# QK-norm attention and a SiLU feed-forward on one core: three more couples of heads loaded in 32-row quarters and transposed on VectorE

## The chip, the core and the metric

The kernel runs on one core of one Trainium2 chip. TensorE (PE in the profile) multiplies matrices and writes PSUM; VectorE (DVE), ScalarE (ACT) and GpSimd (POOL) do the rest; DMAs are issued from queues, nearly all of them here from the SyncE queue (SP). The metric is the time of one execution on the device in microseconds (us); lower is better.

## The reference

```python
def rmsnorm(x, g):                       # over the 64 columns of a head
    return x / np.sqrt(np.mean(x * x, axis=-1, keepdims=True) + 1e-06) * g
q_n, k_n = rmsnorm(q, g_q), rmsnorm(k, g_k)       # (8, 12, 448, 64) each
scores = (1 / 8) * np.matmul(q_n, k_n.transpose(0, 1, 3, 2))
attn = softmax(scores)                            # + 1e-9 in the denominator
attn_out = np.matmul(attn, v)
x = attn_out.transpose(0, 2, 1, 3).reshape(3584, 768)
h = x @ w_in                                      # w_in (768, 2048)
out = (h / (1 + exp(-h))) @ w_out                 # w_out (2048, 768)
```

q, k, v and the gains are float32. `w_in` and `w_out` come as 64-bit floats, which the kernel loads as pairs of 32-bit words and rounds to float32 itself.

## The kernel before

**Couples.** The 12 heads of each of the 8 batches are worked on four at a time. Such a set of four heads is a *couple*; there are 24 (`NC`), three to a batch, so couple c belongs to batch c // 3. The main loop of `bounded` runs over c and calls `visit(c)` and then `between(c)`.

`visit(c)` holds the attention matmuls of couple c: `scores` (keys by queries into a PSUM tile `sc`, then ScalarE's Exp, L731) alternates with `weigh` (exponentials by v, L763). It also divides the couple before by its softmax sums (`divide`, L824), and in some couples it rounds a piece of `w_in` (`weights_in_visit`).

`between(c)` prepares couple c + 1 and fills TensorE's time with the feed-forward of two batches that are finished. It runs `fill` twice. A `fill` takes a fixed number of steps of the feed-forward's matmuls (L923; one step is one float32 product of 448 columns, two instructions in the trace): 13 steps in couples 6 to 11, 14 from couple 12 on. Among these steps `fill` deals out other work by hand: a list `others`, spread evenly over the steps, and a list `prompt`, of which one entry is issued at once and one more after every third step. The matmuls are those of a seven-product scheme (`Seven`): products 1, 2, 6, 5, 7, 3, 4 of three steps each make one block; product 5 is copied to a `stage` slot by ScalarE (L941), product 1 too (L931), the others are added by VectorE (L873), GpSimd adds two parts (L943, L944), and when a block is done ScalarE applies SiLU (L1061) and SP stores it to `hidden` (L956). There are three `stage` slots, so product 5 of a block goes into a slot whose store must have landed.

**Two ways to normalise and transpose.** Before the scores, q and k must stand with the 64 columns of a head on partitions.

- Couples 6 to 11, below `LATE` (12): q is loaded by rows (L266, two DMAs of 224 KB) and k by rows (L292, L296, four DMAs). Squares are taken by ScalarE (L470) and summed by VectorE (L471); GpSimd takes the power -1/2 (L499) and multiplies q (L514); for k the factor is used later as the scale of the Exp. `transpose_q` is 8 TensorE transposes (L643) and a ScalarE copy of 128x896 (L647); `transpose_k` is 7 transposes (L661) and a ScalarE copy that applies the gains (L663).
- Couples from `LATE` on: q is loaded in 32-row quarters (`load_quarters`, L253, eight DMAs of 56 KB with runs of 32 floats), and k twice, by rows for its squares (L285, L287, six DMAs) and in quarters (L253, eight more). v comes in plain token order (L312, L323, L325: eight DMAs instead of four). `flip` transposes 32x32 blocks on VectorE (L669 for q, L672 for k); `gain` applies the gains to k (ScalarE, L678). The squares of q are one ScalarE instruction (`sum_squares`, L686) and one VectorE sum (L687); `scale` adds the two halves of a head with a small TensorE matmul (L698), and VectorE (L699) and GpSimd (L702 power, L705 multiply) finish. `pair_up` changes the identity matrix for that matmul once, two couples ahead.

In the `between` of these late couples the second `fill` has this list of prompts: the first reciprocal of the softmax sums (L808) at once; the second and its spreading DMAs (L815, L817) after step 3; `flip(c + 1, "k")` and the load of the next quarters after step 6; `gain` and `sum_squares(c + 2)` after step 9. After the last step `scale(c + 2)` is issued, so its matmul L698 stands on TensorE between the feed-forward and the scores of `visit(c + 1)`. The weight steps of that `fill` are dealt in its first half, since as many empty entries are put behind them.

**Buffers and banks.** From couple 8 on, q has one buffer, so the load of the next q is issued behind the transposition of the present one. The places `k0` and `k1` hold k of even and odd couples below `LATE`; from there on `k0` takes the rows and `k1` the quarters. `bank` gives the feed-forward's products their PSUM: two `mm` banks, and, when `turns["third"]` is set (c >= `LATE` - 1), every other product takes an `sc` tile instead while more than five steps are due.

**The weights.** `w_in` is 24 pieces: a load (L86, SP), an opening by ScalarE (L101, L102; "o" in the table of steps) and a rounding by VectorE (L124, L127, L131) and GpSimd (L135; "r"). The last ones fall into couples 6 to 10, and so do the sums of weight blocks for the seven products (`sum_w_in`, L870 and L873 on W, 128x768): four in the visits of couples 7 and 9, and in couple 10 three in the first `fill` and one in the second. A load into a raw buffer waits on SP until the piece before it there has been rounded.

**The order of the output.** Up to `plain` = 4, batches hold their tokens with every fourth token side by side, and `store` writes a tile of 128 tokens in two or three interleaved DMAs (L533); from batch 4 on in one or two plain ones (L526).

Of the kernel before, what the change touches and what calls it, by code (L numbers as in the profile page):

```python
# [30 lines left out]
class Shapes:  # L31
    def __init__(self, q, w_in):
        self.B, self.H, self.S, self.D = q.shape
        self.DM, self.DFF = w_in.shape
        self.P = 128
        self.J = 4
        self.R = self.S // self.J
        self.NPAIR = self.H // 2
        self.NW = self.DM // self.P
        self.NF = self.DFF // self.P  # L40
        self.HALF = self.DM // 2
        self.FULL = self.S // self.P
        self.REST = self.S - self.FULL * self.P

        self.KEYS = self.S // self.P
        self.LEFT = self.S - self.KEYS * self.P
        assert 2 * self.LEFT == self.P and self.NPAIR % 2 == 0 and self.LEFT == self.D

        self.KA, self.KL, self.KB = 0, 2 * self.KEYS * self.D, 2 * (self.KEYS + 1) * self.D
        self.NK = self.KB + 2 * self.KEYS * self.D  # L50
        assert 2 * self.D == self.P and self.J * self.R == self.S and 2 * self.REST == self.P
        assert self.NW == self.NPAIR and self.B % 2 == 0

        self.LATE = 2 * self.NPAIR
        self.Q = 32
        assert 2 * self.S == self.NK and 4 * self.Q == self.P and self.D == 2 * self.Q

# [136 lines left out]
def kernel(  # L194
# [25 lines left out]
    nc = tc.nc  # L220
    z = Shapes(q, w_in)
# [8 lines left out]
    place, at = {}, 0  # L230
# [16 lines left out]
    def load_quarters(rows, t):  # L247

        rows = rows.rearrange("n (a p) d -> n p a d", p=z.Q)
        for i in range(2):  # L250
            for h, half, quarter in z.quarters():
                dst = t[quarter, ts(i, z.S)].rearrange("p (a e) -> p a e", e=z.Q)
                nc.sync.dma_start(dst, rows[2 * i + h][:, :, ts(half, z.Q)])  # L253
# [18 lines left out]

    def load_k_quarters(c):
        b, cp = divmod(c, z.NPAIR // 2)
        load_quarters(k[b, ts(cp, 4)], place["k1"])

    def load_k(c):
        t = place[f"k{c % 2}"]
        if c >= z.LATE:
            t = place["k0"]  # L280
            for i, start in enumerate((z.KA, z.KB)):
                main, left = plain(k, c, i)
                dst = t[:, ds(start, z.KL)].rearrange("p (j h d) -> p h j d", j=z.KEYS, h=2)
                for h in range(2):
                    nc.sync.dma_start(dst[:, h], main[:, h])  # L285
                dst = t[ds(i * z.LEFT, z.LEFT), ds(z.KL, 2 * D)]
                nc.sync.dma_start(dst.rearrange("p (h d) -> p h d", h=2), left)  # L287
            return
        main, left = keys_of(k, c)
        for i, start in enumerate((z.KA, z.KB)):  # L290
            dst = t[:, ds(start, z.KL)].rearrange("p (j h d) -> p j h d", j=z.KEYS, h=2)
            nc.sync.dma_start(dst, main[:, ts(i, 2)].rearrange("p h j d -> p j h d"))  # L292
            if i == 0:
                for m in range(2):
                    dst = t[ds(m * z.LEFT, z.LEFT), ds(z.KL, 2 * D)]
                    nc.sync.dma_start(dst.rearrange("p (h d) -> p h d", h=2), left[m])  # L296

    def plain(source, c, i):

        b, cp = divmod(c, z.NPAIR // 2)  # L300
        rows = source[b, ds(4 * cp + 2 * i, 2)]
        start = i * z.LEFT
        main = rows[:, ds(start, z.KEYS * P)].rearrange("h (j p) d -> p h j d", p=P)
        return main, rows[:, ds((1 - i) * z.KEYS * P, z.LEFT)].rearrange("h p d -> p h d")
# [56 lines left out]
    norm = Norm(nc, z, rms, minus_half)  # L361
# [177 lines left out]
def bounded(  # L539
# [10 lines left out]
    NC, loads, place, norm, spare, ones, first, squares = (  # L550
        own[name] for name in ("NC", "loads", "place", "norm", "spare", "ones", "first", "squares")
    )
    GROUP, LATE = z.NPAIR, z.LATE
# [13 lines left out]
    def piece(n):  # L567
        nonlocal at
        at += n
        return work[:, at - n : at]  # L570

    qT = piece(2 * S).rearrange("p (i s) -> p i s", i=2)
    kT = piece(z.NK)
# [26 lines left out]
    def q_of(c):  # L600
        return rows_q[c % 2 if c < GROUP + 2 else 0]
# [64 lines left out]
    def flip(c, name):  # L666

        if name == "q":
            nc.vector.transpose(qT.rearrange("p i s -> p (i s)"), q_of(c)[:, 0 : z.NK])  # L669
            load_q(c + 1)  # L670
            return
        nc.vector.transpose(kT, place["k1"])  # L672
        if c + 1 < NC:
            loads["quarters"](c + 1)

# [152 lines left out]
    def normalise(c):  # L828


        def piece(name, i):
            t = scratch[i if c < GROUP + 2 else 0]
            source = raw_of(c) if c < GROUP else q_of(c)
            if name == "q":
                norm.squares_q(c, source, t, i)
            else:
                norm.squares_k(c, place["k0" if c >= LATE else f"k{c % 2}"], t, i)
            if name == "q" and c < GROUP:
                norm.root(c, name, i)
                norm.scale(c, source, q_of(c), i, nc.gpsimd)  # L840
                if i == 1 and c + 2 < GROUP:
                    load_q(c + 2)
            elif i == 1:
                norm.root(c, name)
                if name == "q":
                    for m in range(2):
                        norm.scale(c, source, q_of(c), m, nc.gpsimd)
                elif LATE <= c < NC - 1:
                    loads["k"](c + 1)

        if c >= NC:
            return []
        return [lambda a=a: piece(*a) for a in (("q", 0), ("q", 1), ("k", 0), ("k", 1))]
# [261 lines left out]
    QUADS = NT // 4  # L1115
    QUARTER = z.HALF // 2
# [156 lines left out]
    def save_out(q, i, j):  # L1273
        for t in range(2):
            store(
                nc, out, z, (4 * q + 2 * (i - 1) + t) * P, results[i, j][t], (j - 1) * z.HALF,
                nc.gpsimd if q == QUADS - 1 and i == 2 else nc.sync, plain=4,
            )

    def quad(q):  # L1280
        c = results

        def product(name, out, more):
            n = DEEP.index(name)
            if q > 0 or n >= FIRST:
                deep(name, out, more, DEEP[(n + 1) % len(DEEP)])
                return
            for t in range(2):
                o = single(name, t)
                if more:  # L1290
                    plus(o, out[t], out[t])
                else:
                    nc.scalar.copy(out[t], o)

        first = q == 0
        if first:
            fetch(0, 1, 0)
            sum_deep_right(7)
        product(4, c[2, 1], False)
        if first:  # L1300
            sum_deep_right(4)
        sum_left(0)
        sum_left(2)
        if first:
            sum_deep_right(3)
        product(1, c[1, 1], False)
        for t in range(2):
            nc.scalar.copy(c[1, 2][t], c[1, 1][t])
        sum_left(1)
        if first:  # L1310
            sum_deep_right(6)
            sum_deep_right(1)
        product(2, c[1, 1], True)
        save_out(q, 1, 1)
        if first:
            sum_deep_left(6)
            sum_deep_right(2)
        sum_left(3)
        product(5, c[2, 2], False)
        if first:  # L1320
            owed.extend(lambda i=i: sum_deep_right(5, (i,)) for i in ORDER)
        fetch(q + 1, 1, 1)
        product(6, c[1, 2], True)
        fetch(q + 1, 0, 0)
        product(7, aside, False)
        for t in range(2):
            plus(aside[t], c[1, 2][t], aside[t])
            plus(c[1, 2][t], c[2, 2][t], c[1, 2][t])
            plus(c[2, 2][t], aside[t], c[2, 2][t])
            plus(c[2, 1][t], aside[t], c[2, 1][t])  # L1330
        save_out(q, 2, 2)
        save_out(q, 2, 1)
        fetch(q + 1, 1, 0)
        if q == QUADS - 1:

            def then(t, h):
                store(
                    nc, out, z, (4 * q + t) * P, c[1, 2][t][:, ts(h, QUARTER)],
                    z.HALF + h * QUARTER, *((nc.scalar, nc.sync)[:: 1 if h else -1]), plain=4,
                )  # L1340

            deep(3, c[1, 2], True, None, then)
            return
        product(3, c[1, 2], True)
        save_out(q, 1, 2)
        fetch(q + 1, 0, 1)
# [457 lines left out]
```

## Time and profile before

| | us |
|---|---|
| median of 3 runs | 1311.59 (1311.17 to 1312.17) |
| the profiled execution | 1311.68 |
| its span, first to last instruction | 1309.9 |
| TensorE busy | 1294.2 (99% of the span) |
| VectorE / ScalarE / GpSimd busy | 950.1 / 505.0 / 360.8 |
| DMAs of queue q1 (SP) | 38.8% of 16 engines' span |

Times inside the span are counted from its start. Couple c runs from the first score matmul of `visit(c)` to that of `visit(c + 1)`: couple 7 starts at 150.45, 8 at 184.66, 9 at 218.56, 10 at 251.88, 11 at 287.69, 12 at 319.65. Busy time of TensorE is not throughput: the profile models the ends of matmuls, and one that follows another begins before the modelled end of the first. So the distances between starts are what counts here, and the chain of waits shows these. A queue of an engine (SPq) shows DMA issues, which aren't counted as busy.

### The profile page before, as it was taken

To read this page: it belongs to the slowest core of one execution; us is meant where nothing else is said; L and a number is where in the kernel's file an instruction comes from. 1 tells how busy PE (TensorE), PEld (TensorE's weight loads), DVE (VectorE), ACT (ScalarE), POOL (GpSimd) and SP (SyncE) were. 2 spreads that over 40 slices of the span, in tenths; PEclk is the share of its full clock that TensorE was granted. 3 is DMA by queue.
4 is the path that set the end of the run, shared out by engine and by line. 5 is a ranking of instruction groups with operands and counts; after the bars stand their busy time and mean duration, and the time that the engine had idled before them with its cause. 6 is when DMAs were issued, how large, how long until landed. Compare 5 with 4: busy or idle time off the path is not lost.

```text
span 1309.9 us, 19866 instructions
## 1 busy us (share of the span) xinstructions
PE 1294.2 (99%) x7209; PEld 832.3 (64%) x7209; DVE 950.1 (73%) x1627; ACT 505.0 (39%) x886; POOL 360.8 (28%) x230
## 2 busy tenths in 40 slices
PE   9999999999999999999999999999999999999998
PEld 4444444444444444444444455558999999999998
DVE  6998777777655556755554786698978787878785
ACT  7866656645544545545544354310000000100000
POOL 6766544453334333334320244300000000000000
PEclk9999999999999999999999999999999999999999
DMA  9674335344443444444321457312323223231411
GB/s 242 169 198 121 100 98 164 113 95 110 108 94 90 121 96 95 98 113 95 83 68 63 141 191 253 125 61 78 106 81 101 85 95 110 68 127 52 136 42 40
DMA packets 249439, 144.94 MB, mean 111 GB/s; under 512 B 184292, under 2 KB 233220, under 8 KB 249332
## 3 DMA queue, kind: packets, MB, share of 16 engines
q1 hardware_dynamic: 248672, 142.42, 38.8%
q8 instruction: 59, 0.97, 0.3%
q0 software_dynamic: 352, 0.96, 0.2%
q14 instruction: 48, 0.39, 0.1%
q10 hardware_dynamic: 308, 0.20, 0.1%
HBM read 93.98 MB, written 41.29 MB: 103 GB/s over the span
## 4 chain that ended last, share of the span: by engine, by line
PE 94%; DVE 2%; ACT 2%; issue 1%; POOL 0%; ACTq 0%; DVEq 0%; POOLq 0%
PE alone L1230 23%; PE mm L923 22%; PE av L763 9%; PE sc L726 9%; PE sc L923 9%; PE mm L1230 8%; PE alone L923 7%; PE alone L1267 2%; PE sc L799 1%; PE mm L799 1%; PE mm L1267 1%; PE sc L643 1%; PE sc L661 1%; ACT work L731 1%; DVE work L777 0%
## 5 line engine op out<-in xcount | busy, mean ns | idle before, releaser
L731 ACT ACTIVATE work<-sc,rms 128x448 f32<-128x448 f32 x318 | 181.1, 634 | 63.1 <-PE sc L726 50.4
L923 PE MATMUL mm<-x,W 128*128 128x448 f32 x414 | 169.9, 545 | 4.0 <-DVE parts L873 1.8
L726 PE MATMUL sc<-work 64*64 64x448 f32 x1344 | 164.1, 544 | 1.8 <-ACT work L731 1.5
L777 DVE TENSOR_TENSOR work<-work 128x896 f32<-128x896 f32 (+1 forms) x114 | 124.6, 1125 | 50.0 <-PE av L763 49.5
L923 PE MATMUL mm<-sums_x,W 128*128 128x448 f32 x372 | 152.5, 543 | 0.5 <-DVE parts L873 0.5
L763 PE MATMUL av<-work,rows 64*64 64x448 f32 x1272 | 150.7, 540 | 0.5 <-DVE av L739 0.3
L499 POOL TENSOR_TENSOR rms<-rms,minus_half 128x14 f32<-128x14 f32 (+4 forms) x43 | 105.4, 2453 | 148.2 <-DVE rms L495 138.6
L923 PEld LDWEIGHTS mm<-x,W 128*128 128x128 f32 x414 | 76.4, 190 | 87.2 <-issue 73.7
L526 POOL DMA_DIRECT2D out_dram<-x x2 | 1.2, 592 | 443.3 <-DVE x L873 443.3
L923 PEld LDWEIGHTS mm<-sums_x,W 128*128 128x128 f32 x372 | 69.2, 190 | 73.7 <-issue 68.0
L1230 PE MATMUL alone<-W,rows 128*128 128x192 f32 x610 | 113.0, 326 | 0.0
L763 PEld LDWEIGHTS av<-work,rows 64*64 64x64 f32 x1272 | 57.8, 132 | 69.1 <-issue 33.8
L1230 PEld LDWEIGHTS alone<-W,rows 128*128 128x128 f32 x610 | 101.5, 190 | 0.0
L726 PEld LDWEIGHTS sc<-work 64*64 64x64 f32 x1344 | 52.9, 132 | 74.1 <-ACT work L731 30.8
L943 POOL TENSOR_TENSOR parts<-parts,stage 128x448 f32<-128x448 f32 x31 | 41.9, 1351 | 146.7 <-DVE parts L873 146.3
L923 PE MATMUL sc<-x,W 128*128 128x448 f32 x198 | 80.6, 543 | 0.0
L702 POOL TENSOR_TENSOR rms<-rms,minus_half 128x28 f32<-128x28 f32 x12 | 57.5, 4792 | 61.7 <-DVE rms L699 61.7
L1230 PE MATMUL alone<-W,work 128*128 128x192 f32 x382 | 72.2, 326 | 0.0
L1061 ACT ACTIVATE stage<-stage 128x896 f32<-128x896 f32 x63 | 57.3, 945 | 21.9 <-DVE stage L873 21.0
L1240 ACT COPY rows<-alone 128x192 f32<-128x192 f32 x33 | 10.5, 318 | 141.6 <-PE alone L1230 78.2
L1230 PEld LDWEIGHTS alone<-W,work 128*128 128x128 f32 x382 | 63.8, 190 | 0.0
L923 PEld LDWEIGHTS sc<-x,W 128*128 128x128 f32 x198 | 36.9, 190 | 39.6 <-issue 37.2
(259 smaller groups left out, 2283.6 us busy)
## 6 DMA issues: line engine op xcount, KB each, us to landing
hidden<-stage SPq DMA_DIRECT2D x63, 448.0 KB, 3.2
work<-hidden SPq DMA_DIRECT2D x21, 1024.0 KB, 5.1
rows<-in_moe_w_out_dram SPq DMA_DIRECT2D x32, 384.0 KB, 3.3
W<-in_moe_w_in_dram SPq DMA_DIRECT2D x22, 512.0 KB, 5.2
x<-hidden SPq DMA_DIRECT2D x7, 1024.0 KB, 6.4
work<-work SPq DMA_DIRECT2D x111, 56.0 KB, 2.0
rows<-in_q_dram SPq DMA_DIRECT2D x96, 56.0 KB, 2.2
rows<-in_k_dram SPq DMA_DIRECT2D x96, 56.0 KB, 2.2
```

The source lines that it names most:

```text
L499: nc.gpsimd.tensor_tensor(out=t, in0=t, in1=half, op=ALU.pow)
L702: nc.gpsimd.tensor_tensor(out=f, in0=f, in1=minus_half.to_broadcast([P, n]), op=ALU.pow)
L726: nc.tensor.matmul(two[ds(half * D, D), h, 0:S], keys[rows, ts(half, D)], qT[rows, pair, :], start=True, stop=True,)
L731: nc.scalar.activation(left_weights(c)[:, h] if j == LEFT else weights(c, j)[:, i, h], two[:, h, 0:S], AF.Exp, scale=norm.column(c, i, h, j),)
L763: nc.tensor.matmul(sums[i][ds(h * D, D), :], v, w, start=(j == 0 and step == 1), stop=(j == LEFT - 1 and step == 1),)
L777: nc.vector.tensor_tensor(out=total, in0=total, in1=more, op=ALU.add)
L799: nc.tensor.matmul(t[ds(h * D + i * n, n), :], ones[:, which + i if which else 0], left_weights(c)[:, h] if which else w()[:, i, h], start ...
L923: nc.tensor.matmul(t, self.left(name, s), self.right(name, s), start=s == ends[0], stop=s == ends[1])
L943: nc.gpsimd.tensor_tensor(out=u2, in0=u2, in1=p5, op=ALU.add)
L1061: nc.scalar.activation(t, t, AF.Silu)
L1230: nc.tensor.matmul(t, x[:, i], y, start=i == ORDER[0], stop=i == ORDER[-1])
L1267: nc.tensor.matmul(o, a[:, 2 * i + m, t], right_one(name, i)[:, m], start=n == 0, stop=n == len(steps) - 1,)
```

## The change

`LATE` goes from 12 to 9, and `plain` from 4 to 3, so that couples 9, 10 and 11 (batch 3) take the second way above and are stored in plain token order. Since 9 is odd, the two places of k change roles. `pair_up` moves from couple 10 to 7, the first `flip` from `between(11)` to `between(8)`, the first `sum_squares` and `scale` from `between(10)` to `between(7)`, the use of the `sc` tiles for products from couple 11 to 8, and the dealing of weight steps in the first half of the second `fill` applies to couples 7 to 9 too. All of this follows from `LATE`; `flip`, `gain`, `sum_squares`, `scale` and `fill` themselves are as before.

```diff
-        self.LATE = 2 * self.NPAIR
+        self.LATE = 3 * self.NPAIR // 2
+        self.PLAIN = 3
+        self.BY_ROWS, self.BY_QUARTERS = f"k{self.LATE % 2}", f"k{1 - self.LATE % 2}"
...
     def load_k_quarters(c):
         b, cp = divmod(c, z.NPAIR // 2)
-        load_quarters(k[b, ts(cp, 4)], place["k1"])
+        load_quarters(k[b, ts(cp, 4)], place[z.BY_QUARTERS])
...
         if c >= z.LATE:
-            t = place["k0"]
+            t = place[z.BY_ROWS]
...
-        nc.vector.transpose(kT, place["k1"])
+        nc.vector.transpose(kT, place[z.BY_QUARTERS])
...
-                norm.squares_k(c, place["k0" if c >= LATE else f"k{c % 2}"], t, i)
+                norm.squares_k(c, place[z.BY_ROWS if c >= LATE else f"k{c % 2}"], t, i)
...
-                nc.gpsimd if q == QUADS - 1 and i == 2 else nc.sync, plain=4,
+                nc.gpsimd if q == QUADS - 1 and i == 2 else nc.sync, plain=z.PLAIN,
...
-                    z.HALF + h * QUARTER, *((nc.scalar, nc.sync)[:: 1 if h else -1]), plain=4,
+                    z.HALF + h * QUARTER, *((nc.scalar, nc.sync)[:: 1 if h else -1]), plain=z.PLAIN,
```

## The prediction

> **What bounds the kernel now.** First the busy times on the page:
>
> ```profile
> PE 1294.2 (99%) x7209; PEld 832.3 (64%) x7209; DVE 950.1 (73%) x1627; ACT 505.0 (39%) x886; POOL 360.8 (28%) x230
> ```
>
> TensorE is never free, so a matmul taken away is worth its time unless TensorE then waits. VectorE's 73% is an average; the changed couples need the stretches. From one couple's start to the next (columns: start and end, length, then busy of PE, PEld, DVE, ACT, POOL), couples 8, 9, 10 and 11:
>
> ```profile
> 184.66:218.56 33.90, 33.90 (x188) 16.16 (x188) 24.87 (x35) 21.14 (x35) 15.76 (x10) 1.00 0.43 126
> 218.56:251.88 33.32, 33.32 (x188) 16.40 (x188) 24.92 (x32) 21.24 (x36) 13.30 (x8) 1.00 0.43 126
> 251.88:287.69 35.81, 34.52 (x191) 15.50 (x190) 29.51 (x35) 19.97 (x32) 17.31 (x13) 1.00 0.42 110
> 287.69:319.65 31.96, 31.96 (x176) 15.21 (x175) 18.31 (x24) 15.57 (x25) 12.50 (x7) 1.00 0.35 85
> ```
>
> Couple 11, whose `between` already flips, takes 31.96 us; couples 8, 9 and 10, with TensorE's transposes, take 33.90, 33.32 and 35.81. But couple 11 has 18.31 us of VectorE work and the others 24.87, 24.92 and 29.51: the rounding and the sums of `w_in` fall there. The chain of waits gives TensorE's share of couple 8 (start, length, what):
>
> ```profile
> 195.72 0.92 PE sc L643 x8
> 196.64 9.79 PE mm L923 x26
> ...
> 206.43 0.76 PE sc L661 x7
> 207.19 0.89 PE sc L799 x8
> 208.08 10.55 PE mm L923 x26
> ```
>
> A `fill` of 13 steps takes 9.75 us undisturbed (26 x 0.375). The transposes are 0.92 + 0.76 = 1.68 us.
>
> Now the chain that replaces them, from the timeline of couple 11 (start, length, engine, line):
>
> ```profile
> 314.54 1.06 DVE L672 STREAM_TRANSPOSE work<-rows 128x896 f32<-128x896 f32 x1
> ...
> 315.63 1.04 ACT L678 ACTIVATE work<-work,gains 128x896 f32<-128x896 f32 x1 [2.24 <-DVE work L672]
> ...
> 316.58 0.94 ACT L686 ACTIVATE rows<-rows 128x896 f32<-128x896 f32 x1
> ...
> 317.54 1.09 DVE L687 TENSOR_REDUCE rms<-rows 128x28 f32<-128x896 f32 x1 [1.44 <-ACT rows L686]
> ...
> 319.42 0.30 PE L698 MATMUL sc<-rms,ident 128*128 128x28 f32 x2
> ```
>
> Flip, gain, square and sum follow one another across two engines, 314.54 to 318.63, and TensorE's L698, which stands before the next scores, needs the sum. With no weight work at all in couple 11 the slack is 319.42 - 318.63 = 0.8 us. This is the place to watch. Last, the SP queue and its followers in couple 8:
>
> ```profile
> 193.59 3.50 SPq L86 DMA_DIRECT2D W<-in_moe_w_in_dram  x2
> ...
> 199.70 2.14 SPq L266 DMA_DIRECT2D rows<-in_q_dram  x2
> 201.93 1.10 SPq L956 DMA_DIRECT2D hidden<-stage  x2
> ```
>
> ```profile
> 206.07 0.53 ACT L941 COPY stage<-mm 128x448 f32<-128x448 f32 x1 [3.12 <-DMA hidden<-stage]
> ...
> 206.50 0.63 ACT L470 ACTIVATE rows<-rows 128x512 f32<-128x512 f32 x1
> ...
> 209.11 1.55 DVE L808 RECIPROCAL work<-sc 128x224 f32<-128x224 f32 x1
> ```
>
> SP stands at L86 until GpSimd has rounded a piece (193.56), then issues without a pause; the store L956 comes last, and ScalarE's copy of product 5 (L941) has waited 3.1 us for it to land.
>
> **What is removed and added on TensorE.** `between` of couples 8, 9 and 10 loses 1.68 us each, 5.04. L698 is added in couples 7, 8 and 9; in couple 10 it takes 287.46 to 287.69, 0.23 us, so +0.69. Sum -4.35 us. The Trainium skill (TensorE: Matmul & The Clock Gate, Part 4) gives about 275 ns for a transpose in one kernel's context; the row's 273 ns for a single L661 looks the same, but these overlap and start 109 ns apart. By the page as an estimate 45 transposes would be worth 12.4 us.
>
> An undisturbed changed couple: visit 11.0 (184.73 to 195.72), two fills 19.5, softmax sums L799 0.89, L698 0.23: 31.62. Couple 11's 31.96 shows 0.34 of small waits.
>
> **ScalarE** loses per couple L647 0.91, L663 1.00 and two q squares 1.25 and gains L678 1.04 and L686 0.93: 1.2 us less, worth nothing by itself. **VectorE** loses two q sums and a scalar step (0.68 + 0.68 + 0.17) and gains 1.10 + 1.06 + 1.09 + 0.19: 1.9 us more. **GpSimd**: 4.8 + 1.7 for 2.9 + 2.8, 0.8 more, while it is busy under half of these couples. The third bank lets TensorE run one or two products (2.25 us each) ahead of evictions; I cost it at nothing, since couple 11 pays 0.34 in all with it, and one product, 2.25, if a score must wait for its tile.
>
> **SP.** A load in quarters is eight issues, in the later couples
>
> ```profile
> 264.42 4.32 SPq L253 DMA_DIRECT2D rows<-in_q_dram  x8
> ```
>
> against 2.14 for L266. v takes 2.4 + 1.9 us (couple 11: 291.76 to 294.2, 297.84 to 299.76) for 1.8 + 0.6. On couple 8's list, L86 ends at 197.1; then 2.4 + 1.9 + 4.2 put the store at about 205.7 instead of 201.93. Queued behind it are the next L86, k's rows, the spread, k's quarters. The Trainium skill (DMA: Bandwidth & Descriptors, Specifications) wants runs of 512 B or more and speaks against quarters of 128 B; the trace shows them landing in 2.2 us median, and the rule would lengthen landings only, adding no term here.
>
> **Where the stalls go.**
>
> *Couple 8.* A store landing 4.1 us after its issue, as before, lets L941 start at 209.9, 3.9 late. Behind L941 on ScalarE stand the squares of k, and VectorE's sums of them stand before the reciprocals, so L808 starts at 213.0. From there by the rows: reciprocal to 214.5, eviction 215.0, reciprocal 216.5, GpSimd's parts (L499, then L943) 216.9, eviction 217.5, flip 218.6, gain 219.6, square 220.5, sum 221.8, L698 222.1. TensorE, having started 0.23 late and lost two sets of transposes, would be there at 216.5: a stall of 5.6, in place of the 0.8 now. Bounds: 0.3 (couple 11's small waits, if the quarters don't hold up SP) and 7.2 (a store landing in 5.7, the longest row). I take 5.6, for this very wait is in the trace. ScalarE then applies SiLU and loads the Exp table late, first Exp some 3.3 us after the scores; couple 10 starts so now and its visit takes 11.86 instead of 10.99: 0.87 lost in visit 9 (bounds 0 and 1.5).
>
> *Couple 9.* SP has room again. In the second fill the copy L931, SiLU with its table load and three weight openings of 1.3 us (L101 and L102) are ahead of `gain`. Now L799 starts at 241.0, L931 at 245.97, and SiLU ends at 249.6, so at +8.6; the last opening +9.95, gain +11.0, square +11.95, sum +13.05; TensorE is ready at +10.64. Stall 2.4; from 0.3 (couple 11) to 4 (VectorE: first flip and rounding ahead of L672 end it near +10.6, sum at +13.7, and a little lateness from couple 8). Now 0.25. The late Exp of visit 10 (0.87) disappears: ScalarE loads the table while TensorE stands.
>
> *Couple 10.* VectorE is dense from 255.94 to 280.49, the end of the second reciprocal. With flip q 1.1 more: 4.06 + 24.55 + 1.1 = 29.7 after the couple's start, which is 9.0 after L799's; eviction, flip +10.65, gain, square, sum +13.7, against 10.64. Stall 3.2; from 0.3 to 4.5 (nothing of the 0.6 us gaps absorbed). The present 1.28 there (L941 behind a store that SP issues at 282.87) goes.
>
> Couple 7 gets `pair_up` (0.99 on GpSimd, now hidden in the 5.4 us that GpSimd waits in couple 10, then in the 12.6 us before 170.3 or beside TensorE's second fill; 0.99 if L943 has to wait for it) and the first `sum_squares`, without flip or gain ahead of it: ScalarE has done its openings by 179.0, square and sum end by about 182, L698 comes at 184.7 (0 to 1 us, if VectorE's rounding and evictions come first). It keeps its loads in time: rows of k, quarters, then the spread ends near 185.3 instead of 183.0, lands by about 187.2, and `divide` starts at 188.74.
>
> *Sum.* Couple 8: 31.62 + 5.6 = 37.2; couple 9: 31.62 + 0.87 + 2.4 = 34.9; couple 10: 31.62 + 3.2 = 34.8; 106.9 against 103.03, and 0.23 in couple 7: **+4.1 us**. The fewer plain stores of quads 2 and 3 are worth 0: TensorE's products run there without a gap, and SP has idle time between stores. The profiled execution took 1311.68 (span 1309.9 and 1.8 around it), 0.1 above the median: 1311.68 + 4.1 = **1315.8**.
>
> **Rivals.**
>
> 1. *Everything hides: faster.* One mechanism: the third bank and emptier ScalarE keep the chain flip-to-sum ahead of TensorE in couples 8 to 10, as in couple 11. It decides if L672 starts no later than 6.5 us after L799 (10.64 minus the 4.1 of couple 11). Then 3 x 31.96 + 0.23 - 103.03 = -6.9; with 1.5 us left in couple 8, -5.4: 1306.3. For it: couples 12 on (14 steps) always meet L698 in time. Against: their slack comes from a fourteenth step and no weight work.
> 2. *Half of it.* Only SP's delay: 37.2 + 0.87 + 2 x 31.96 = 102.0, -0.8 net: 1310.9. Only VectorE's and ScalarE's chains: 31.96 + 34.0 + 34.8, -2.0: 1309.7.
> 3. *Worse.* The spread, behind rows and quarters on SP, lands after `divide` is due, and DMAs at 1.03 busy share (203 to 207 us) slow every landing: upper bounds 7.2, 1.5, 4, 4.5 over 3 x 31.62 give +9.3: 1321.
> 4. *The change doesn't reach.* Excluded: every use of the second way hangs on `LATE`.
>
> **How the numbers follow.** My forecast 0.55 (own range 1312.9 to 1319), rival 1 0.20, rival 2 0.18, rival 3 0.07. The time is the forecast's, 1315.8. The range 1306.5 to 1319.8 leaves about half of rival 1 and most of rival 3 outside. A difference under 0.2% (2.6 us) can't be told from none here: faster means below 1309.0, rival 1 and a quarter of rival 2: 0.24. Same, 1309.0 to 1314.2: the rest of rival 2 and the forecast's low end: 0.20. Slower 0.56.
>
> **What would show it.** Right: in couple 8 the store near 205.7, L941 waiting for it till about 210, L698 waiting for L687 (no L698 waits for VectorE now), couples 8 to 10 near 37, 35 and 35 us. Wrong: L687 done before L698's turn; couples 8 to 10 near 32; or a store that is issued before the quarters of q.

## The result and the profile after

| | before | after |
|---|---|---|
| median (6 runs each) | 1311.53 us (1311.17 to 1312.17) | 1317.28 us (1315.68 to 1317.70) |
| ratio, 95% interval | | 1.0037 (1.0026 to 1.0048) |
| span of the profiled execution | 1309.9 | 1315.9 |
| start of couple 12 | 319.65 | 325.62 |

The change is slower, by 5.75 us of the median. The line numbers of the changed kernel are higher by 2 (L253 is now L255, L726 is L728, L923 is L925, L941 is L943); those of single experiments shift by a few more. The page of the changed kernel gives the busy times:

```profile
PE 1293.3 (98%) x7170; PEld 830.8 (63%) x7170; DVE 952.9 (72%) x1630; ACT 502.3 (38%) x880; POOL 365.1 (28%) x227
```

39 TensorE instructions have gone (7209 to 7170: 45 transposes less, three times the two instructions of the matmul L698 more), and the kernel lost time all the same. So TensorE waits somewhere. The stretches of couples 8 to 11 of the changed kernel say where (columns as before: stretch, length, busy of PE, PEld, DVE, ACT, POOL, clock, DMA share, GB/s):

```profile
184.92:224.66 39.74, 35.32 (x175) 16.15 (x174) 26.99 (x35) 19.87 (x32) 17.47 (x9) 0.91 0.44 114
224.66:258.67 34.01, 32.44 (x175) 15.14 (x174) 28.02 (x35) 22.09 (x36) 14.83 (x7) 1.00 0.55 143
258.67:293.66 34.99, 32.25 (x176) 15.28 (x175) 29.28 (x35) 16.82 (x27) 16.59 (x8) 1.00 0.42 102
293.66:325.62 31.96, 31.96 (x176) 15.22 (x175) 18.32 (x24) 15.59 (x25) 13.48 (x7) 1.00 0.44 100
```

| couple | before | after | predicted |
|---|---|---|---|
| 7 | 34.21 | 34.89 | 34.44 |
| 8 | 33.90 | **39.74** | 37.2 |
| 9 | 33.32 | 34.01 | 34.9 |
| 10 | 35.81 | 34.99 | 34.8 |
| 11 | 31.96 | 31.96 | 31.96 |

Couple 12 starts 5.97 later and the span ends 6.0 later: couple 8 loses 5.84, couple 9 0.69 and couple 7 0.68, and couple 10 gives 0.82 back, 6.39 in all. The other 0.42 lies ahead of the changed couples: couple 7 starts at 150.03 in this execution and at 150.45 in the one before, and in the profiles of all versions between 149.96 and 151.87.

Couple 7's 0.68 is L700's 0.23 and a wait behind `pair_up` (L713), which now stands ahead of GpSimd's addition L945; VectorE waits for that addition, and TensorE for VectorE:

```profile
180.92 0.99 POOL L713 COPY ident<-ident 32x32 f32<-32x32 f32 x4
...
181.99 1.13 POOL L945 TENSOR_TENSOR parts<-parts,stage 128x448 f32<-128x448 f32 x1
...
183.15 0.62 DVE L875 TENSOR_TENSOR stage<-mm,parts 128x448 f32<-128x448 f32 x1 [2.08 <-POOL parts L945]
...
183.83 1.02 PE L925 MATMUL mm<-x,W 128*128 128x448 f32 x2 [0.29 <-DVE stage L875]
```

Couple 8 is the only one of these four with a granted clock below 1 (the number 0.91 in its row). Its timeline in the changed kernel (start, length, engine, line; in brackets the idle time before and what ended it):

```profile
203.52 4.05 SPq L255 DMA_DIRECT2D rows<-in_q_dram  x8
...
207.67 0.90 SPq L958 DMA_DIRECT2D hidden<-stage  x2
...
208.43 2.42 PE L925 MATMUL sc<-x,W 128*128 128x448 f32 x6
...
210.55 0.53 ACT L943 COPY stage<-mm 128x448 f32<-128x448 f32 x1 [8.06 <-DMA hidden<-stage]
...
213.59 1.55 DVE L810 RECIPROCAL work<-sc 128x224 f32<-128x224 f32 x1
...
217.23 4.82 PE L925 MATMUL sc<-x,W 128*128 128x448 f32 x6 [3.57 <-DVE work L810]
...
221.06 1.09 DVE L689 TENSOR_REDUCE rms<-rows 128x28 f32<-128x896 f32 x1
...
221.84 2.76 PE L925 MATMUL mm<-x,W 128*128 128x448 f32 x6
...
224.43 0.30 PE L700 MATMUL sc<-rms,ident 128*128 128x28 f32 x2
```

Read it from the top. SP issues the eight quarters of q, and only then the store of `hidden` (L958), at 207.67 instead of 201.93. ScalarE's copy of product 5 has waited 8.06 us for that store's landing. What stands behind it is late in turn: the squares of k, their sums, the reciprocals of the softmax sums. The second reciprocal ends at 217.08, and only then is the `sc` tile free in which TensorE is to put its next product: it has stood for 3.57 us. Six matmuls of that product take 4.82 us; the same six took 2.42 at 208.43. The stretches around that wait show why (clock: the number before the last two):

```profile
211.00:213.70 2.70, 2.52 (x6) 1.06 (x6) 1.43 (x4) 1.95 (x5) 0.00 (x0) 1.00 0.88 262
213.70:217.20 3.50, 0.00 (x0) 0.00 (x1) 3.38 (x3) 0.29 (x1) 3.44 (x2) 0.78 0.39 88
217.20:222.10 4.90, 4.87 (x7) 2.45 (x8) 4.57 (x7) 1.90 (x3) 2.61 (x3) 0.50 0.23 59
222.10:224.70 2.60, 2.60 (x12) 1.26 (x11) 0.04 (x1) 2.58 (x4) 0.00 (x0) 0.92 0.58 104
```

After the idle stretch TensorE is granted half its clock for some 5 us. Each of the six timed executions has its mean granted clock on record: four have 0.996 to 0.998 and take 1317.19 to 1317.70 us, two have 0.999 and take 1315.68 and 1315.73. So the lower clock seems not to have come in every execution; only the first of the six was profiled. The chain of waits of the changed kernel leads back through the same places:

```profile
207.10 0.48 SPq L255
207.57 0.05 issue
207.67 2.78 DMA hidden<-stage
...
210.98 0.64 ACT rows L472
...
213.59 1.55 DVE work L810
...
217.23 4.82 PE sc L925 x6
```

In couples 9 and 10 the timeline of TensorE shows these waits:

```profile
258.37 0.38 PE L700 MATMUL sc<-rms,ident 128*128 128x28 f32 x2 [1.36 <-DVE rms L689]
282.31 2.52 PE L925 MATMUL sc<-x,W 128*128 128x448 f32 x6 [1.74 <-DVE stage L875]
288.09 2.49 PE L925 MATMUL sc<-sums_x,W 128*128 128x448 f32 x6 [1.00 <-DVE work L810]
293.43 0.30 PE L700 MATMUL sc<-rms,ident 128*128 128x28 f32 x2
```

In couple 9 (the first line), L700 waits for the sum L689. In couple 10 (the other three) it doesn't: there two products wait for their banks.

### The profile page after: what moved, and what is told of

It reads as the page before. It is cut to its first block, busy times and chain, and to the rows that moved or that the text cites. A ratio compares the mean times of both kernels' runs of the same rounds, so it can differ in the third digit from the quotient of the medians.

```text
span 1315.9 us, 19881 instructions
## 1 busy us (share of the span) xinstructions
PE 1293.3 (98%) x7170; PEld 830.8 (63%) x7170; DVE 952.9 (72%) x1630; ACT 502.3 (38%) x880; POOL 365.1 (28%) x227
## 4 chain that ended last, share of the span: by engine, by line
PE 90%; DVE 5%; ACT 2%; issue 2%; DMA 1%; POOL 1%; SPq 0%; ACTq 0%; DVEq 0%; POOLq 0%
PE alone L1232 23%; PE mm L925 17%; PE sc L925 10%; PE av L765 10%; PE sc L728 9%; PE mm L1232 8%; PE alone L925 7%; PE alone L1269 2%; PE mm L801 1%; DVE work L779 1%; PE sc L801 1%; PE mm L1269 1%; DVE work L810 1%; PE sc L645 0%; ACT work L733 0%
## 5 line engine op out<-in xcount | busy, mean ns | idle before, releaser
L728 PE MATMUL sc<-work 64*64 64x448 f32 x1344 | 163.6, 543 | 1.3 <-ACT work L733 1.0
L925 PE MATMUL mm<-x,W 128*128 128x448 f32 x372 | 153.8, 546 | 3.8 <-DVE parts L875 1.3
L925 PE MATMUL mm<-sums_x,W 128*128 128x448 f32 x354 | 145.7, 544 | 1.0 <-DVE parts L875 0.5
L501 POOL TENSOR_TENSOR rms<-rms,minus_half 128x14 f32<-128x14 f32 (+4 forms) x40 | 96.0, 2402 | 139.8 <-DVE rms L497 135.7
L925 PEld LDWEIGHTS mm<-x,W 128*128 128x128 f32 x372 | 69.0, 191 | 79.6 <-issue 69.1
L925 PEld LDWEIGHTS mm<-sums_x,W 128*128 128x128 f32 x354 | 65.9, 190 | 72.0 <-issue 66.1
L925 PE MATMUL sc<-x,W 128*128 128x448 f32 x240 | 100.1, 554 | 5.3 <-DVE work L810 3.6
L728 PEld LDWEIGHTS sc<-work 64*64 64x64 f32 x1344 | 53.2, 132 | 71.2 <-ACT work L733 30.2
L704 POOL TENSOR_TENSOR rms<-rms,minus_half 128x28 f32<-128x28 f32 x15 | 71.9, 4793 | 69.8 <-DVE rms L701 63.4
L945 POOL TENSOR_TENSOR parts<-parts,stage 128x448 f32<-128x448 f32 x31 | 41.9, 1351 | 147.1 <-DVE parts L875 146.7
L925 PEld LDWEIGHTS sc<-x,W 128*128 128x128 f32 x240 | 45.6, 193 | 54.4 <-issue 49.4
```

The lines of the kernel that those rows point to most:

```text
L501: nc.gpsimd.tensor_tensor(out=t, in0=t, in1=half, op=ALU.pow)
L704: nc.gpsimd.tensor_tensor(out=f, in0=f, in1=minus_half.to_broadcast([P, n]), op=ALU.pow)
L728: nc.tensor.matmul(two[ds(half * D, D), h, 0:S], keys[rows, ts(half, D)], qT[rows, pair, :], start=True, stop=True,)
L925: nc.tensor.matmul(t, self.left(name, s), self.right(name, s), start=s == ends[0], stop=s == ends[1])
L945: nc.gpsimd.tensor_tensor(out=u2, in0=u2, in1=p5, op=ALU.add)
```

## The experiments

The lengths of couples 8 to 10, the start of couple 12 and the span come from each kernel's profiled execution; the ratio is that of its timed runs to the kernel before on the same chip. All edits act behind the start of couple 7, which lies between 149.96 and 150.73 in these executions and at 151.87 in e6; by so much the starts of couple 12 and the spans differ without the edits. The couples' lengths are free of it.

| | couple 8 | 9 | 10 | start of 12 | span | ratio to before |
|---|---|---|---|---|---|---|
| before | 33.90 | 33.32 | 35.81 | 319.65 | 1309.9 | |
| after | 39.74 | 34.01 | 34.99 | 325.62 | 1315.9 | 1.0037 [1.0026, 1.0048] |
| e1 | 35.63 | 34.00 | 34.99 | 321.74 | 1312.3 | 1.0017 [1.0007, 1.0026] |
| e2 | 39.28 | 33.99 | 32.43 | 322.66 | 1313.0 | 1.0024 [1.0015, 1.0034] |
| e3 | 39.49 | 34.55 | 35.95 | 327.40 | 1318.1 | 1.0051 [1.0035, 1.0068] |
| e4 | 43.55 | 34.01 | 34.98 | 329.63 | 1320.4 | 1.0074 [1.0058, 1.0091] |
| e5 | 39.95 | 33.32 | 35.81 | 325.21 | 1315.7 | 1.0041 [1.0027, 1.0055] |
| e6 | 39.08 | 35.75 | 36.31 | 329.80 | 1324.0 | 1.0098 [1.0081, 1.0115] |
| e7 | 34.14 | 34.41 | 34.98 | 320.71 | 1313.3 | 1.0026 [1.0016, 1.0036] |
| e9 | 33.75 | 38.23 | 34.73 | 324.27 | 1318.2 | 1.0060 [1.0044, 1.0077] |
| e10 | 34.16 | 34.00 | 34.99 | 320.29 | 1310.7 | 1.0006 [0.9997, 1.0015] |
| e12 | 34.57 | 33.97 | 36.68 | 322.21 | 1312.6 | 1.0009 [1.0000, 1.0018] |
| e13 | 34.12 | 33.98 | 34.67 | 319.79 | 1310.0 | 1.0004 [0.9995, 1.0013] |
| e14 | 33.99 | 33.99 | 34.66 | 320.01 | 1310.2 | 1.0011 [1.0002, 1.0020] |

**e1: couple 10's q behind the store.** The load is issued after the first `fill` of `between(8)`, behind the flip that empties its buffer.

```diff
-            load_q(c + 1)
+            if c != LATE:
+                load_q(c + 1)
...
+        if c == LATE - 1:
+            load_q(c + 2)
```

> The changed kernel, but in couple 8 the eight loads of couple 10's q are issued after the first fill instead of ahead of the hidden store. Queue theory (couple 8 loses because the store stands behind v and q on SP): the store is issued near 203.6 instead of 207.67, L943 starts near 206.7 instead of 210.55, the wait for the sc tile shrinks below 1 us and the clock does not drop; couple 8 takes 33 to 34.5 us instead of 39.74, couples 9 and 10 stay at 34 to 35, the kernel ends 5 to 6.5 us earlier, near the time of the kernel before. Rival (VectorE's own extra 1.9 us in couple 8 is what fills it): couple 8 stays above 38 us, total within 1 us of the changed kernel.

The store is issued at 204.02, the copy of product 5 starts at 207.42 after 4.70 of waiting, and couple 8 is 4.11 shorter. The queue is the cause, and not VectorE's extra work, which is all still there. But 1.7 more than before is left, and the timeline of TensorE in e1 shows where:

```profile
214.10 2.49 PE L926 MATMUL sc<-x,W 128*128 128x448 f32 x6 [0.74 <-DVE work L811]
216.43 2.42 PE L926 MATMUL mm<-x,W 128*128 128x448 f32 x6
220.46 0.41 PE L701 MATMUL sc<-rms,ident 128*128 128x28 f32 x2 [1.61 <-DVE rms L690]
```

The moved q now lands late for its own squares, which L690 sums: its last quarter lands at 218.01, and the squares start at 218.34. Both this q and the store are wanted at the same time, from one queue. No six matmuls of a product take longer than 2.49 in this couple.

**e5: the kernel before, with the longer issues alone.** Nothing is flipped; only couple 10's q goes out as eight DMAs and couple 9's v as eight.

```diff
+        if c == 10:
+            for i in range(2):
...
+                for h in range(2):
+                    for half in range(2):
+                        nc.sync.dma_start(dst[:, :, h, d], src[:, :, h, d])
...
+        if c == 9:
+            for n in range(4):
+                nc.sync.dma_start(dst[:, n], main[:, n, 0 : z.KEYS - 1])
...
```

The part left out cuts the last rows of v, one DMA, into two.

> The kernel before (TensorE's transposes, two banks, no flips in couples 8 to 10), with one thing of the change: the loads that stand ahead of the hidden store on SP in couple 8 are cut into as many issues as the change has there (couple 10's q in eight issues with runs of 32 floats instead of two, couple 9's v in four and four instead of one and three); same bytes, same places. Queue theory: the store is issued 3.5 to 4.5 us later than 201.93, L941 starts near 210 instead of 206.07, TensorE stands in couple 8, which takes 36.5 to 39 us instead of 33.90; total 2.5 to 5 us more than the kernel before. Rival (the flips' chain makes the loss, and a late store alone is hidden as the 3.1 us wait in the kernel before is): couple 8 at most 34.5 us, total within 0.7 us of the kernel before.

Its timeline of couple 8:

```profile
202.54 5.40 SPq L270 DMA_DIRECT2D rows<-in_q_dram  x8
208.04 1.03 SPq L973 DMA_DIRECT2D hidden<-stage  x2
...
211.22 0.53 ACT L958 COPY stage<-mm 128x448 f32<-128x448 f32 x1 [8.75 <-DMA hidden<-stage]
...
211.80 4.85 PE L940 MATMUL mm<-x,W 128*128 128x448 f32 x6 [3.26 <-ACT stage L958]
```

Ten more issues ahead of the store, and no other edit, make couple 8 39.95 us: the whole loss of couple 8 without the change. The wait shows at another place, since two banks are in use here and the product behind product 5 waits for ScalarE's copy itself; and the slow product after it, 4.85 instead of 2.42, is here too.

**e7: couple 8's two stores from ScalarE's queue.**

```diff
-        nc.sync.dma_start(hidden[f, :, ds(column, t.shape[1])], t)
+        queue = nc.scalar if filler.get("couple") == LATE - 1 else nc.sync
+        queue.dma_start(hidden[f, :, ds(column, t.shape[1])], t)
...
+        filler["couple"] = c
```

> The changed kernel with couple 8's two hidden stores issued from ScalarE's queue, right after its SiLU, instead of SP's; nothing else is moved. Queue theory: the store goes out near 201.5, L943 starts by 206.5, no wait for the sc tile over 1 us, granted clock 1.00, and the chain's end and TensorE meet: couple 8 takes 32.5 to 34.5 us instead of 39.74; total 5 to 7 us less, about the time of the kernel before. Rival (landing is slow since the DMA engines are at their limit there, wherever the store is issued): L943 still after 209, couple 8 above 38.

The store goes out at 203.81 and 205.23 (201.5 was expected), the copy starts at 207.00 without a wait, couple 8 is 34.14. The end doesn't follow: couple 12 starts 1.06 later than before and the last VectorE instruction comes 1.07 later (1305.38 for 1304.31), but the span is 3.4 longer. The other 2.3 lie behind that last instruction, 7.6 us of tail instead of 5.2. e6 and e9, of the same series on that chip, have long tails too (7.2 and 6.8); e5 beside them and all the others have 5.2 to 5.6. What makes it stays open.

**e10: couple 10's q from GpSimd's queue.**

```diff
-    def load_quarters(rows, t):
+    def load_quarters(rows, t, queue=nc.sync):
...
-            load_quarters(rows, t)
+            load_quarters(rows, t, nc.gpsimd if c == z.LATE + 1 else nc.sync)
```

> The changed kernel, but couple 10's q quarters are issued by GpSimd instead of SP. Theory (couple 8 pays for SP's eight q issues ahead of the store; GpSimd waits from 198 to 208.7 us there and can issue them for nothing): store of couple 8 near 204.0 as with q behind it, the copy of product 5 near 207.4, and now the squares of q don't wait for q either: couple 8 33.8 to 34.5 us against 39.74, couples 9 and 10 within 0.5 of 34.0 and 35.0, couple 12 starts 320.0 to 320.8. Rival (GpSimd's issues delay its rounding and norm work, and TensorE pays for that): couple 8 over 35.6.

The timeline of e10, couple 8:

```profile
200.21 5.12 POOL L255 DMA_DIRECT2D rows<-in_q_dram  x8 [2.27 <-DVE work L671]
...
203.64 0.91 SPq L958 DMA_DIRECT2D hidden<-stage  x2
...
207.31 0.53 ACT L943 COPY stage<-mm 128x448 f32<-128x448 f32 x1 [4.58 <-DMA hidden<-stage]
...
219.00 0.41 PE L700 MATMUL sc<-rms,ident 128*128 128x28 f32 x2 [0.26 <-DVE rms L689]
```

GpSimd, which in e7 stands idle from 197.9 to 208.7 here, has time for the eight issues, and neither the store nor the squares of q are late. Couple 8 is 34.16, 5.58 less than in the changed kernel, and the ratio to before is 1.0006, with 1 inside the interval; couples 7 to 10 of its profile are together 0.8 longer than before. One queue position is thus the whole measurable loss. It isn't a gain, though: couples 8 to 10 are still 7.3 above three of couple 11's length.

**e2: eight sums of `w_in` left out** (both chunks 2 and 3; the products then use unsummed blocks).

```diff
     def sum_w_in(i, step):
...
+        if i >= 2:
+            return
```

> The changed kernel, leaving out the sums of w_in's last two chunks (eight VectorE instructions of 128x768: four in visit 9, four in couple 10), so the output is not the reference's. VectorE theory for couples 9 and 10: couple 10 falls from 34.99 to 32 to 32.8, couple 9 from 34.01 to 32.5 to 33.5 (ScalarE's openings and SiLU ahead of the gain remain); couple 8 stays at 39.7; total 3 to 4.5 us less. Rival (SP's queue or the DMAs also set couples 9 and 10): both stay within 0.5 us of 34.01 and 34.99.

Couple 10 falls from 34.99 to 32.43, as expected: its waits are VectorE's density. Couple 9 stays at 33.99, which was a miss: VectorE isn't what holds it.

**e3: the third bank from couple 11 on only.**

```diff
-        turns["third"] = c >= LATE - 1
+        turns["third"] = c >= 2 * GROUP - 1
```

> The changed kernel with the sc tiles used for products from couple 11 on, as in the kernel before, instead of from couple 8. Theory 'the borrowed tile is a new wait' (product 1 of couple 8 waits for the tile that the softmax sums hold until the second reciprocal): without it couple 8 is at most 38 us and total 1 to 2 us less. Rival 'the third bank helps, and the chain of late k squares sets the end anyway': with two banks products 3 and 4 wait as well, couple 8 takes 40 to 43 us, couples 9 and 10 0 to 1 us more, total 0 to 4 us more.

Couple 8 is 39.49 with two banks and 39.74 with three. TensorE then waits 2.68 for product 5's copy instead of 3.57 for the reciprocal, and its next product again takes 4.22 us for 2.42. So the borrowed tile moves the wait but isn't its cause. Couples 8 to 10 are 1.25 longer in all with two banks, but couple 10's 35.95 holds a stretch at about half clock (see the last section), so what the third bank is worth isn't shown.

**e4: sixteen extra matmuls in couple 8's second fill**, to keep TensorE from standing.

```diff
+            if turns.get("busy") and steps == 7:
+                for _ in range(16):
+                    nc.tensor.matmul(turns["free"][:, 1, 0:P], ident, ident, start=True, stop=True)
...
```

> The changed kernel with 16 extra float32 matmuls of 128 columns (about 3.5 us of TensorE's time, results unused) in couple 8 after product 4, where TensorE stands 3.57 us and the granted clock afterwards is 0.50. Clock theory: without the idle stretch the clock stays at 1.00, product 1 takes 2.25 instead of 4.82 us, and couple 8 is 2 to 2.6 us shorter although TensorE has more work; the next wait is then L700 for the sum L689. Rival (the slow product is slowed by something else, such as the DMAs or VectorE): product 1 still takes 4.8 us and the total is unchanged or 0.5 to 1 us more.

It didn't take the wait away. The timeline of e4:

```profile
218.63 5.47 PE L1372 MATMUL sc<-ident 128*128 128x128 f32 x32 [4.48 <-DVE stage L875]
223.94 2.42 PE L926 MATMUL sc<-x,W 128*128 128x448 f32 x6
```

The extra matmuls write a tile that VectorE has yet to evict, so TensorE stood 4.48 us ahead of them instead of 3.57. One thing can still be read from it: the extra matmuls now take 5.47 us where 3.5 were expected, and product 1 behind them, which took 4.82 in the changed kernel, takes 2.42. What is slow is what follows the wait, and not this product.

**e6: k flipped right after q, gain and squares three steps earlier.**

```diff
-                reciprocals += [lambda: flip(c + 1, "k"), gain]
+                reciprocals += [lambda: (next_k(c + 1), gain(), sum_squares(c + 2))]
...
             flip(c + 1, "q")
+            flip(c + 1, "k")
...
```

> The changed kernel with k's flip on VectorE directly behind q's flip at the start of between, from couple 8 on, and gain and the squares of q three steps earlier; the loads stay where they were. Chain theory (couple 9 loses 2.4 us since gain, square and sum end after TensorE): couple 9 falls from 34.01 to 31.8 to 32.6; couple 8 stays at 38.5 to 40 (store and sc tile come before the chain); couple 10, which waits for banks behind VectorE, falls by at most 1; total 1.5 to 3 us less than the changed kernel. Rival (couple 9 waits for what stands ahead of the chain, so that the order makes no difference): couple 9 within 0.5 of 34.01.

Couples 9 and 10 get longer, to 35.75 and 36.31, and each of couples 13, 16 and 19 by 0.65. In couple 9 of e6:

```profile
257.67 1.09 DVE L691 TENSOR_REDUCE rms<-rows 128x28 f32<-128x896 f32 x1 [1.90 <-ACT rows L690]
...
258.67 0.61 DVE L877 TENSOR_TENSOR stage<-mm,stage 128x448 f32<-128x448 f32 x1
...
259.34 2.01 PE L927 MATMUL mm<-sums_x,W 128*128 128x448 f32 x4 [3.19 <-DVE stage L877]
```

VectorE's sum of squares (L691) now stands ahead of the evictions in VectorE's queue and waits there for ScalarE; TensorE waits for the evictions behind it.

**e9: e6, e7 and the eight sums on GpSimd together.**

```diff
+        if i >= 2:
...
+            nc.gpsimd.tensor_tensor(out=o, in0=x, in1=y, op=op)
+            return
```

> The changed kernel with the stores of e7_store_act, the order of e6_flip_first, and the eight sums of w_in's last two chunks on GpSimd instead of VectorE. If the three losses are separate and these are their causes: couples 8, 9 and 10 take 32 to 33.5 us each, total 4 to 7 us less than the kernel before (1305 to 1308). If GpSimd's sums (about 2 us each by its 1.13 to 1.35 us for 128x448) come too late for the feed-forward's product that needs them, couple 10 takes 34 to 37 us and the total is within 2 us of the kernel before.

Couple 8 is good (33.75) and couple 9 bad (38.23): e6's fault is larger here, 3.92 of waiting at the same place.

**e12 to e14: couple 9's and couple 10's rest.** All three contain e10. e12 deals the last rounding and the last weight opening of couple 9 behind the squares; e13 adds two sums of chunk 3 on GpSimd; e14 deals both last openings behind the squares.

The edit of e12 and e13:

```diff
             steps = weights_in(c, 1)
+            if c == LATE:
+                queries += [steps.pop(1), steps.pop(-1)]
```

In e14 it is this:

```diff
+            if c == LATE:
+                queries += steps[1:]
+                steps = steps[:1]
```

And that of the sums in e13 and e14:

```diff
+        if i == 3 and step < 2:
...
+            nc.gpsimd.tensor_tensor(out=o, in0=x, in1=y, op=(ALU.add, ALU.subtract)[step])
+            return
```

> Couple 10's q quarters by GpSimd as before, and in couple 9's second fill the last rounding step and the last weight opening are dealt behind gain, squares and sum instead of ahead of them. Theory (couple 9's stall of 2.4 is the opening and SiLU on ScalarE and the rounding on VectorE ahead of the flip and gain): gain starts about 1.1 earlier, when SiLU ends, L700's wait for L689 falls from 1.36 to under 0.5, couple 9 32.9 to 33.3 against 34.00; couple 10 35.0 to 35.4. Rival (the wait is set by VectorE's reciprocals, whose end the opening and rounding don't touch): couple 9 stays over 33.7.

> The kernel of the run before, and the first two of the four sums of w_in's last chunk (couple 10) on GpSimd instead of VectorE. Theory (couple 10 waits 1.74 and 1.00 for banks because VectorE is dense up to the second reciprocal; two sums are 2.2 us of it): couple 10 32.8 to 33.8, couple 12 starts 317.5 to 318.6, span 1307.5 to 1309.5. Rival (GpSimd takes 1.8 us for a sum instead of 1.0 and TensorE or VectorE's third sum waits for it): couple 10 34.4 or more.

> The kernel of e13, but in couple 9's second fill both of the last two weight openings (and the rounding between them) are dealt behind gain, squares and sum; in e12 and e13 one opening was still ahead of gain on ScalarE. Theory (ScalarE's opening and SiLU ahead of gain set couple 9's stall; e12 showed that the flip, 1.2 earlier, doesn't): gain starts when SiLU ends, 1.1 earlier, L700's wait for L689 falls from 1.8 to 0.5 to 0.9, couple 9 32.7 to 33.2 against 33.98; if the two openings then hold up the Exp table, visit 10 gives back up to 1 (couple 10 34.6 to 35.7). Couple 12 starts 318.6 to 319.8. Rival (SiLU moves later or something else takes the opening's place): couple 9 stays over 33.7.

None gets couple 9 below 33.97. ScalarE's timeline of e14 shows why:

```profile
245.29 0.53 ACT L933 COPY stage<-sc 128x448 f32<-128x448 f32 x1 [2.57 <-PE sc L925]
245.84 1.28 ACT L1066 ACT_TABLE_LOAD   x1
247.14 1.79 ACT L1066 ACTIVATE stage<-stage 128x896 f32<-128x896 f32 x2
248.84 0.66 ACT L103 ACTIVATE x<-x 128x512 int32<-128x512 uint32 x1
249.39 0.65 ACT L104 ACTIVATE W<-x 128x512 f32<-128x512 f32 x1
249.95 1.03 ACT L680 ACTIVATE work<-work,gains 128x896 f32<-128x896 f32 x1
```

The opening that was left in the list is dealt later when there are fewer of them, and slips again between SiLU and gain. So gain starts 30.5 to 30.6 us after the start of the couple in e10, e12 and e14 alike (249.95 - 219.40 in e14), while the flip of k starts 1.5 earlier in e12 and e14 than in e10 (27.4 after the start, 28.9 in e10). That excludes VectorE's flip and rounding as the bound of couple 9; ScalarE's order from product 1's copy to the gain is left. That taking the opening out of it would give 1.1 us wasn't shown. Couple 10's 36.68 in e12 is the clock's (see the last section). In e13 couple 10 gains only 0.3 on e10: the two sums take 1.8 and 2.6 us on GpSimd, where VectorE takes 0.9 to 1.2 for one, and a product waits 1.25 for them. What moving couple 10's sums into couple 11, where VectorE has only 18.3 us of work, would give was not measured. No version beats the kernel before.

## Why the prediction was right, and where not

The forecast (slower, 1315.8) was right in sign and 1.5 below the measured median; 1317.28 lies in the range. Over couples 7 to 10 the sum had +4.1, and the profiled execution shows +6.39. By couples the forecast was 0.45, 2.54 and 0.19 too low in couples 7, 8 and 10 and 0.89 too high in couple 9, so part of the nearness is luck. That the two executions with a mean clock of 0.999 agree with 1315.8 to 0.1 us rests on the same cancelling.

- **TensorE's work** (-4.35): every transposition of couples 8 to 10 is gone and L700 is there, and couple 11 is unchanged at 31.96. Couple 7 took 0.68 more for 0.23: the wait of L945 (L943 before) behind `pair_up`, which the prediction had named with a price of 0.99 and put at nothing, cost 0.45.
- **Couple 8, the queue.** Each link of the chain was there: store 207.67 (205.7 foretold), copy 210.55 (209.9), first reciprocal 213.59 (213.0), flip 218.01 (217.5), sum done 222.15 (221.8). But the store was 2.0 late, since L88 stood until 198.06 and not 197.1 and v's issues took 5.4 and not 4.3; and the copy began 2.9 behind it and not 4.1. These two errors nearly cancel, which was luck. e1, e5, e7 and e10 show that the place in the queue is the cause.
- **Couple 8, the mis-sized term: the stall of 5.6.** It measured 39.74 - 31.62 = 8.1. The third bank was put "at nothing", with 2.25 as a bound "if a score must wait for its tile"; instead a product waits for its `sc` tile, 3.57 us, and TensorE runs at half clock after it. With two banks couple 8 is as long (39.49 in e3), so the third bank isn't what the sum lacked; the clock is. From 217.23, two products at 2.25 would have brought TensorE to L700 at 221.73. The sum L689 ends at 222.15 and doesn't depend on these two products, and in e10 the next couple starts 0.39 after the end of that sum; so it would have started near 222.5. It starts at 224.66: some 2.1 us, by this estimate, are the clock's. The prediction had no term for them, and without them the couple would have been about 37.6 for 37.2. For the same reason the sign that was named, L698 waiting for L687, didn't show here: L700 came too late to wait for L689.
- **Visit 9.** The 0.87 for a late Exp didn't appear: its scores and `weigh` run from 224.66 in 10.97 us, as in an undisturbed visit. The table was loaded at 225.60, as late as foretold, but the scores began 2.1 later, so the slow products seem to have hidden it; no run here separates the two.
- **Couple 9.** Stall foretold 2.4, measured 34.01 - 31.62 = 2.39; L700's wait for L689 shows 1.36 of it. That it comes from ScalarE's order is left by exclusion (e2, e12, e14).
- **Couple 10.** Stall foretold 3.2, measured 3.37, from VectorE's density (e2: -2.56 without the sums). But TensorE pays at two banks, 1.74 and 1.00, and not at L700.
- **The rivals.** Rival 1 needed L674 within 6.5 us of L801 in all three couples; it came 11.3 behind it in couple 8 (218.01 for 206.69). Rival 3's bound for couple 8, 7.2, was exceeded (8.1), by the clock and not by slower landings: the store landed in 2.8.

## What to carry to other kernels

When a load is cut into more DMAs, look at what stands behind it in its queue and not only at the load: here eight issues of half a microsecond put a store back by 4 us, three engines waited in a row for it, and giving the issues to an engine that was idle brought back nearly all of it. Cost a stall of TensorE at more than its length when it is like those of the next section, since the clock may be lower after it: here some 2 us on top of 3.57. A difference of 2 us between two versions can be this alone, so look at the granted clock of each execution before explaining it. An instruction that is put earlier in an in-order queue must not have to wait there, or everything behind it waits as well (e6), and work that is dealt out evenly moves when the list gets shorter (e14).

## What the runs showed of the hardware

The granted clock falls after idle stretches that are shorter than we had expected to matter, and not each time. In the profiles of this case, between 20 and 1280 us, eight waits of TensorE are 2.68 us or longer (2.68 in e3, 3.19 and 3.39 in e6, 3.26 in e5, 3.57 in the changed kernel and e2, 3.92 in e9, 4.48 in e4 ahead of the extra matmuls). After each of them the mean granted clock from 1 to 4 us behind the restart was 0.50 to 0.57. Fourteen waits are 1.61 to 1.81 us long; two of them were followed by such a stretch, twelve by 1.00. No wait of 1.56 us or less was. One of the two is in e3: 1.67 us ahead of couple 10, and then the stretch from 1.0 us after the start of L700 (24 matmuls in 3.1 us at 0.53).

```profile
259.19 0.38 PE L700 MATMUL sc<-rms,ident 128*128 128x28 f32 x2 [1.67 <-DVE rms L689]
```

```profile
260.20:263.30 3.10, 3.10 (x24) 1.07 (x20) 0.00 (x0) 1.16 (x2) 3.10 (x1) 0.53 0.82 151
```

The other is in e12. e12 and e13, whose couples 9 are the same, have the same wait there, 1.80 and 1.81 us before L700, and their stretches from 1.0 us after the start of L700 read, e12 first:

```profile
254.30:257.40 3.10, 3.10 (x24) 1.16 (x20) 0.96 (x3) 1.45 (x4) 2.63 (x2) 0.54 0.86 182
```

and e13:

```profile
253.90:257.00 3.10, 3.10 (x40) 1.25 (x36) 1.12 (x4) 1.98 (x6) 2.64 (x2) 1.00 0.84 176
```

24 matmuls in 3.1 us against 40: the same work lost time once and nothing the other time. That explains e12's couple 10, 36.68 against 34.99 in e10, which has the same sums. It is a matter of the execution: of e12's eleven timed runs, six have a mean granted clock of 0.999 or 1.000 and spans of 1310.1 to 1311.2, and five have 0.997 or 0.998 and spans of 1312.3 to 1312.8. What decides it in one execution stays open. No edit took the wait of couple 8 away with all else left in place; in e1 and e10, where it is 0.74 and 0.62, the product behind it takes 2.49 us at a clock of 1.00.

The Trainium skill (TensorE: Matmul & The Clock Gate, section "Why this matters for your kernels") asks for no idle gaps above about 3 us between bursts of matmuls, and says that one window of idle brings the clock back to half. The half clock agrees with 0.50; the limit is too wide for these runs, where 2.68 us (e3) and once each 1.67 us (e3) and 1.80 us (e12) were enough.
